# Attention, a dense layer and a mixture of experts: a third expert picked ahead of the full ranking

## The chip, the cores and the metric

The kernel runs on one core of a Trainium2 chip, as one launch. The metric is the device time of that launch in microseconds. A shorter time is better. A profile is one execution of the program recorded by the hardware; its span runs from the first to the last instruction.

## The reference

Three layers follow one another: attention over 2 x 8 heads of 768 x 64, a dense layer of 512 -> 2048 -> 512 on 1536 tokens, and a mixture of 8 experts of 512 -> 1024 -> 512, in which each token goes to one expert.

```python
scores_l = where(|i - j| < 16, q @ k.T / 8, -1e9)         # local keys
scores_s = q @ max_of_32(k).T / 8 + log(32)               # 24 summary keys
x = softmax([scores_l, scores_s]) @ [v, mean_of_32(v)]    # -> [1536, 512]

h = x @ w_in                                              # dense layer
x = (h * clip(h + 3, 0, 6) / 6) @ w_out

e = argmax(x @ w_gate); p = softmax(x @ w_gate)[e]        # expert of each token
out = p * (maximum(x @ w1[e], 0) @ w2[e])
```

All data are float32. The kernel writes each product of float32 matrices as three products of float16 halves (high x high, high x low, low x high).

## The kernel before, in words

The work is one long program for five engines, with the order of most steps planned by hand: `POS` and the second argument of `at` give each step a position, and the steps are traced in that order. A scheduler then places the instructions in each engine's program; inside `tc.manual_schedule` the order on the named engines is the written one. A `tc.If` is a conditional block; each engine that has instructions in it evaluates the condition itself, and jumps past the block when it is false.

Attention and the dense layer take the first 377 us. The dense layer's first matmuls are L486 (weights `wih`, `wil`), its second ones L506 (`wo`); `x2_out` stores the result of 128 tokens and transposes it, and `gate` (L526 to L571) picks the expert of each token and writes the token's number into that expert's table `tbl`.

The experts are worked through by rank, the most frequented first. `early` looks at the counts of the first 8 of the 12 token tiles (`PRE`) and fixes the experts of ranks 0 and 1, so that their weights can be loaded and split while the dense layer still runs. `ranking` orders all eight once every token is counted, with the experts picked early kept in front. `s_tile(v, j)` computes tile j (128 tokens, or 64 in a half tile) of rank v: L709 with `w1`, relu on ACT (L713) and the low half on DVE (L714), L728 (L724 in a half tile) with `w2`, the scaling by p (L731, L733) and a scatter to `out` (L734).

Weights come in pieces of 512 KB, eight to an expert (four of `w1`, four of `w2`). `s_load` brings a piece into a raw buffer, by a DMA on SP's queue (L655, L658); `s_split` makes the high half on ACT (L193) and the low half on DVE (L194). Up to the ranking there are three raw buffers (`eraw`), behind it five (`raw`, `RAW`); a load into a buffer follows the split that frees it. Pieces 8 v + i of ranks 0 and 1 are steps `sw0` to `sw15`. Rank 2 and later ranks are prepared by `prep`, four pieces at a time, as `work` inside `s_tile`: there the order on ACT and DVE is written, relu, low half, relu, low half, then the pieces. Rank v's weights lie in pair `v % 4` of `sp["w"]`; two pairs (`w1t`, `w2t`) exist early, two more (`w1u`, `w2u`) are made behind the dense layer.

The order behind the dense layer is: tiles (0,0), (0,1), (0,2) of rank 0, whose rows were gathered early; then a block L876 (`redo`) for the case that rank 0 has fewer tiles than were worked ahead; the half tile of rank 0 if it has one; a nest of blocks L867 with further tiles of rank 0; tile (1,0); a nest L867 with further tiles of rank 1, in the first of which the pieces of ranks 2 to 4 are prepared; then the other ranks. Each tile's tokens come by a gather on GpSimd (L679) and a transposing DMA on SP's queue (L681); each table by a DMA on SP's queue (L673, L784).

In the profiled execution rank 0 has three tiles and a half tile, rank 1 seven tiles, rank 2 a tile and a half tile, ranks 3 and 4 a half tile each.

Of the kernel before, what the change touches and what calls it, by code (L numbers as in the profile page):

```python
# [20 lines left out]
NT = B * S  # L21
# [10 lines left out]
RAW = 5  # L32

# [116 lines left out]
def attn_moe_moe2(ctx, tc, q, k, v, w_in, w_out, w_gate, w1, w2, cf_d, ch_d, out):  # L150
# [17 lines left out]

    wctx = ExitStack()
# [18 lines left out]
    wih = wpool.tile([128, KD, DFF], F16, name="wih")  # L188
    wil = wpool.tile([128, KD, DFF], F16, name="wil")
# [390 lines left out]
    esc = const.tile([1, 5], F32, name="esc")  # L580
    esi = const.tile([1, 4], I32, name="esi")
    early_tiles = [(0, 1), (0, 2)]
    z0, z1 = ew[:, 0, :], ew[:, 1, :]

    def early():

        n, c = ew[:, 2, :], ew[:, 3, :]
        ve.tensor_copy(n, counts(PRE))
        for i, z in enumerate((z0, z1)):
            ve.tensor_reduce(out=esc[:, i:i + 1], in_=n, axis=AX.X, op=ALU.max)  # L590
            ve.scalar_tensor_tensor(out=c, in0=n, scalar=esc[:, i:i + 1], in1=rev[0:1], op0=ALU.is_ge, op1=ALU.mult)
            ve.tensor_reduce(out=esc[:, 2 + i:3 + i], in_=c, axis=AX.X, op=ALU.max)
            ve.tensor_scalar(out=z, in0=rev[0:1], scalar1=esc[:, 2 + i:3 + i], scalar2=None, op0=ALU.is_equal)
            if i == 0:
                ve.scalar_tensor_tensor(out=n, in0=z, scalar=-BIG, in1=n, op0=ALU.mult, op1=ALU.add)
        ve.tensor_scalar(out=esc[:, 2:4], in0=esc[:, 2:4], scalar1=-1.0, scalar2=float(E), op0=ALU.mult, op1=ALU.add)
        ve.tensor_copy(esi, esc[:, 0:4])
        ve.tensor_scalar(out=esi[:, 0:1], in0=esi[:, 0:1], scalar1=7, scalar2=None, op0=ALU.logical_shift_right)
        ve.tensor_scalar(out=esc[:, 4:5], in0=esi[:, 0:1], scalar1=float(len(early_tiles) + 1), scalar2=None, op0=ALU.min)
        return esi  # L600

    def ranking(up):
# [13 lines left out]
        for i, z in enumerate((z0, z1)):  # L616
            ve.scalar_tensor_tensor(out=o, in0=z, scalar=float(2 - i) * 2 * E * NT, in1=o, op0=ALU.mult, op1=ALU.add)
# [21 lines left out]
        ve.scalar_tensor_tensor(out=resi[:, 1:2], in0=esc[:, 4:5], scalar=float(1 << 20), in1=wd[:, 1:2],  # L639
# [97 lines left out]
    def s_open():  # L737
# [5 lines left out]
                   for i in range(2)]  # L743
        xg = {vj: fp.tile([128, 2 * KD, 128], F16, name=f"xe{vj[0]}{vj[1]}") for vj in [(0, 0)] + early_tiles}
# [6 lines left out]
    def tiles_max(v):  # L751

        n, late = PRE * 128, NT - PRE * 128
        if v < 2:
            n = n // (v + 1) + late
        else:
            n = (n * (v - 1) // (v + 1) + late) // (v - 1)
        return -(-n // 128)

    def sparse():  # L760
# [4 lines left out]
        sp["w"] += [(fb.tile([128, 2, KD, FF], F16, name=f"w1u{i}"), fb.tile([128, 2, FK, DM], F16, name=f"w2u{i}"))  # L765
                    for i in range(2)]
# [24 lines left out]
        def raw_loads(first, *gs):  # L791
            with tc.issue_after(first.ins):
                for g in gs:
                    s_load(2, g)
# [18 lines left out]
        def prep(r, half):  # L813

            def piece(i):
                s_split(r, i)
                g = 8 * r + i + RAW
                if g < 8 * E:
                    s_load(g // 8, g % 8)
            return [lambda i=i: piece(i) for i in range(4 * half, 4 * half + 4)]  # L820

        def prep_x(r):
            gather(r, 0)
            h_gather(r)
            if r + 1 < E:
                t_load(r + 1)
                h_load(r + 1)
# [3 lines left out]
        for vj in early_tiles:  # L831
            s_tile(*vj, work=prep(2, 0) if vj == early_tiles[-1] else ())
# [5 lines left out]
        beside = 5  # L838

        def prep_now(r, half):  # L840
            if half == 0 or r == 2:
                prep_x(r)
            for f in prep(r, half):
                f()

        def full(v, j):

            gather(v, j + (2 if v == 1 else 1))
            if (v, j) == (1, 0):
                h_gather(1)  # L850
            if v == 1 and j < beside:
                r, h = 2 + (j + 1) // 2, (j + 1) % 2
                if h == 0 or r == 2:
                    prep_x(r)
                s_tile(v, j, work=prep(r, h))
            else:
                s_tile(v, j)
# [24 lines left out]
        last_half(0)  # L882
        chain(0, n)
# [4 lines left out]
        with tc.If(nt[1] <= 2 * beside - 1):  # L888
            for j in range(1, beside):
                with tc.If(nt[1] <= 2 * j + 1), tc.If(nt[2 + (j + 1) // 2] > 0):  # L890
                    prep_now(2 + (j + 1) // 2, (j + 1) % 2)
        with ExitStack() as st:  # L892
            for v in range(2, E):
# [4 lines left out]
                if v + 3 < E:  # L898
                    with tc.If(nt[v + 3] > 0):  # L899
                        for half in range(2):  # L900
                            prep_now(v + 3, half)
# [118 lines left out]
    def s_early():  # L1020
# [3 lines left out]
        sp["e"] = [reg(esi[0:1, 2 + i:3 + i], E - 1, (ET.SP,)) for i in range(2)]  # L1024
# [7 lines left out]
    def s_early_w(v, i):  # L1032
        s_split(v, i)
        n = 8 * v + i + 3
        if n < 16:
# [3 lines left out]
    for n in range(16):  # L1039
        at(111.9 + n // 2, f"sw{n}", lambda n=n: s_early_w(n // 8, n % 8))  # L1040
# [11 lines left out]
    s_tile(0, 0)  # L1052
# [37 lines left out]
```

## Time and profile before

| what | value |
|---|---|
| median of 3 runs | 565.24 us (558.17 to 565.33) |
| the profiled execution's own time | 560.59 us |
| its span | 558.7 us |
| TensorE (PE) busy | 475.8 us, 85% of the span |
| VectorE (DVE) busy | 304.1 us, 54% |
| ScalarE (ACT) busy | 264.1 us, 47% |
| GpSimd (POOL) busy | 223.3 us, 40% |
| DMA traffic | 87.46 MB, 157 GB/s on average |
| mean granted TensorE clock | 0.928 of full speed |

Sums of a term are made against the profiled execution. A share of busy time is an average over stages; a stage is read by its own window.

### The profile page before, as it was taken

What the parts mean: (1) busy time and instruction counts of PE and PEld (TensorE: products, weight loads), DVE (VectorE), ACT (ScalarE), POOL (GpSimd) and SP (SyncE); (2) the same over time, 40 slices, a digit from 0 to 9 for tenths busy, and PEclk for the clock granted to TensorE, in tenths of its full rate; (3) what the DMA queues carried; (4) which work ended last, traced back from release to release, by engine and by line L of the source; (5) the groups of instructions that cost most, each with busy time, mean ns of one, the idle gap of its engine ahead of it and who ended that gap; (6) DMA issues with size and microseconds to landing.
All of it is one profiled execution on the core that took longest, in us unless ns stands there. A gap on an engine that the chain in (4) does not pass through costs nothing. (4 is left out here: it accounts for less than half of the span.)

```text
span 558.7 us, 12697 instructions
## 1 busy us (share of the span) xinstructions
PE 475.8 (85%) x4792; PEld 324.4 (58%) x4792; DVE 304.1 (54%) x772; ACT 264.1 (47%) x559; POOL 223.3 (40%) x217
## 2 busy tenths in 40 slices
PE   6726966959989999999999997999978969986971
PEld 2325854737656554597578566637745737754650
DVE  5999699996992233645154338954242446320110
ACT  3777685776874213447165406642142346320120
POOL 3476666775675112456245405612213213120110
PEclk8856896898999999999999999999989989997996
DMA  8997977996641354533532348861476999970210
GB/s 272 265 253 192 326 202 161 212 219 181 181 108 34 76 95 105 106 98 58 114 67 50 58 138 248 259 204 40 167 160 172 237 284 328 239 245 22 46 34 7
DMA packets 114773, 87.46 MB, mean 157 GB/s; under 512 B 85199, under 2 KB 94671, under 8 KB 114688
## 3 DMA queue, kind: packets, MB, share of 16 engines
q1 hardware_dynamic: 104656, 65.27, 47.9%
q10 hardware_dynamic: 7056, 13.11, 7.9%
q0 software_dynamic: 2976, 8.01, 4.3%
q8 instruction: 46, 0.75, 0.6%
q14 instruction: 39, 0.32, 0.2%
HBM read 57.29 MB, written 7.97 MB: 117 GB/s over the span
## 5 line engine op out<-in xcount | busy, mean ns | idle before, releaser
L486 PE MATMUL hps<-xt,wih 128*128 128x256 f16 x768 | 136.2, 282 | 9.2 <-DVE rel L492 4.6
L506 PE MATMUL x2ps<-wo,gt 128*128 128x512 f16 x576 | 131.6, 380 | 1.3 <-POOL gt L497 1.1
L486 PE MATMUL hps<-xt,wil 128*128 128x256 f16 x384 | 108.1, 282 | 2.8 <-POOL wil L243 2.8
L506 PEld LDWEIGHTS <-gt 128*128 128x128 f16 x576 | 54.7, 98 | 62.3 <-POOL gt L497 1.6
L486 PEld LDWEIGHTS <-wih 128*128 128x128 f16 x768 | 76.2, 101 | 23.6 <-issue 3.8
L497 POOL TENSOR_TENSOR gt<-rel,gt 128x512 f16<-128x512 f32 x48 | 56.5, 1185 | 39.8 <-ACT gt L496 37.0
L709 PEld LDWEIGHTS <-w1t 128*128 128x128 f16 x1152 | 61.8, 100 | 11.8 <-DVEq L876 4.6
L728 PE MATMUL yp<-w2t,hh 128*128 128x512 f16 x240 | 55.8, 387 | 7.2 <-ACT hh L713 7.0
L714 DVE SCALAR_TENSOR_TENSOR hh<-hp,hh 128x512 f16<-128x512 f32 (+1 forms) x30 | 18.4, 618 | 68.5 <-ACT hh L713 68.4
L492 DVE SCALAR_TENSOR_TENSOR rel<-rel,hps 128x512 f32<-128x512 f32 x48 | 32.6, 680 | 27.9 <-ACT rel L491 27.7
L407 ACT ACTIVATE s<-s,nm 128x184 f32<-128x184 f32 x88 | 38.2, 435 | 19.1 <-DVE nm L402 18.5
L728 PEld LDWEIGHTS <-hh 128*128 128x128 f16 x264 | 25.3, 99 | 36.7 <-ACT hh L713 7.4
L486 PEld LDWEIGHTS <-wil 128*128 128x128 f16 x384 | 38.8, 101 | 10.9 <-POOL wil L243 2.9
L491 ACT ACTIVATE rel<-hps,brelu 128x512 f32<-128x512 f32 x48 | 32.5, 677 | 19.6 <-PE hps L486 14.3
L713 ACT ACTIVATE hh<-hp 128x512 f16<-128x512 f32 (+1 forms) x30 | 16.0, 539 | 54.2 <-PE hp L709 52.3
L709 PE MATMUL hp<-xb,w1t 128*128 128x128 f16 x672 | 38.7, 219 | 1.7 <-DVEq L867 1.7
L496 ACT ACTIVATE gt<-rel 128x512 f16<-128x512 f32 x48 | 29.8, 624 | 20.2 <-DVE rel L492 19.9
L417 POOL TENSOR_TENSOR pb<-s,pb 128x512 f16<-128x512 f32 x22 | 25.9, 1177 | 31.5 <-issue 22.7
L734 POOL DMA_INDIRECT out_dram<-y,tb x8 | 9.2, 1146 | 62.2 <-ACT y L731 40.8
L381 PEld LDWEIGHTS <-qt 64*128 64x128 f16 x576 | 18.6, 100 | 24.3 <-issue 8.8
L569 POOL DMA_INDIRECT tbl<-row,slot x12 | 12.8, 1069 | 45.6 <-DVE slot L563 44.8
L381 PE MATMUL ps<-kb,qt 64*128 64x160 f16 x288 | 19.1, 254 | 10.4 <-DVE nm L397 8.3
(180 smaller groups left out, 783.9 us busy)
## 6 DMA issues: line engine op xcount, KB each, us to landing
raw<-in_moe_w_dram SPq DMA_DIRECT2D x29, 512.0 KB, 6.2
stg<-in_moe_w_out_dram ACTq DMA_DIRECT2D x16, 512.0 KB, 4.2
eraw<-in_moe_w_dram SPq DMA_DIRECT2D x16, 512.0 KB, 4.2
stg<-in_moe_w_in_dram ACTq DMA_DIRECT2D x9, 512.0 KB, 5.0
x2d<-x2c SPq DMA_DIRECT2D x12, 256.0 KB, 2.5
vraw<-in_v_dram SPq DMA_DIRECT2D x11, 256.0 KB, 3.6
qraw<-in_q_dram SPq DMA_DIRECT2D x10, 256.0 KB, 3.6
ek<-in_k_dram SPq DMA_DIRECT2D x3, 512.0 KB, 6.4
```

The lines of the kernel that those rows point to most:

```text
L381: nc.tensor.matmul(out=ps[i % 2][:, o + c0:o + c1], lhsT=qt[u][p, a, h // 2, :], rhs=keys[p, c, h // 2, :], start=(j == 0), stop=(j == 2))
L407: nc.scalar.activation(s[:, i, :], s[:, i, :], AF.Exp, bias=nm[:, i:i + 1], accum_out=sums[u][:, 4 * g + i:4 * g + i + 1])
L417: nc.gpsimd.tensor_tensor(out=p[:, :, 256:384], in0=s[:, :, 0:c1], in1=p[:, :, 0:c1], op=ALU.subtract)
L486: nc.tensor.matmul(out=hps[:, c, :], lhsT=w[:, kk, f:f + 128], rhs=xt[j][:, a * KD + kk, :], start=(i == 0), stop=(i == 3 * KD - 1))
L491: nc.scalar.activation(r, hf, AF.Relu, scale=S_G / (S_X * S_WI) ** 2, bias=brelu)
L492: nc.vector.scalar_tensor_tensor(out=r, in0=r, scalar=6.0 * S_G / (S_X * S_WI), in1=hf, op0=ALU.min, op1=ALU.mult)
L496: nc.scalar.activation(gh, r, AF.Copy)
L497: nc.gpsimd.tensor_tensor(out=gl, in0=r, in1=gh, op=ALU.subtract)
L506: nc.tensor.matmul(out=o, lhsT=gts[j][:, a, f, i * 128:(i + 1) * 128], rhs=w[:, f, :], start=(f == 0 and n == 0), stop=(f == KF - 1 and n ...
L709: nc.tensor.matmul(out=hp[:, c, :], lhsT=w1t[:, a, kk, f:f + 128], rhs=x[:, b * KD + kk, 0:n], start=(i == 0), stop=(i == 3 * KD - 1))
L714: ve.scalar_tensor_tensor(out=hh[:, 1, m * 4:m * 4 + 4, :], in0=hp, scalar=0.0, in1=hi, op0=ALU.max, op1=ALU.subtract)
L728: nc.tensor.matmul(out=yp, lhsT=hh[:, a, f, :], rhs=w2t[:, b, f, :], start=(f == 0 and i == 0), stop=(f == FK - 1 and i == 2))
```

## The change

`EARLY = 3` experts are picked from the counts of the first 8 token tiles instead of 2. The third one's weights go into the space of `wih` and `wil`, which the dense layer's first matmuls have read for the last time by then (they move to a pool of their own, `wi`, that stays open); one pair `w1u`, `w2u` is made later instead of two. Of its eight pieces, 16 and 17 are steps `sw16`, `sw17` behind `sw15`, 18 to 21 are the `work` of tile (0,0), and 22 and 23 (`SOON` = 22) that of tile (0,2), which had 16 to 19. Pieces 24 to 26 are prepared between rank 0's half tile and the nest L867 of rank 0. The rank-1 tiles (1,0) to (1,4) then prepare 3, 3, 3, 2 and 2 pieces, where each had four. The gathers for ranks 2, 3 and 4 are begun in (1,0), (1,1) and (1,3) as before.

```diff
+EARLY = 3
+SOON = 8 * (EARLY - 1) + 6
...
+    wi = ctx.enter_context(tc.tile_pool(name="wi", bufs=1))
...
-    wih = wpool.tile([128, KD, DFF], F16, name="wih")
-    wil = wpool.tile([128, KD, DFF], F16, name="wil")
+    wih = wi.tile([128, KD, DFF], F16, name="wih")
+    wil = wi.tile([128, KD, DFF], F16, name="wil")
...
-    z0, z1 = ew[:, 0, :], ew[:, 1, :]
+    zs = [ew[:, i, :] for i in range(EARLY)]
...
-        for i, z in enumerate((z0, z1)):
+        for i, z in enumerate(zs):
             ve.tensor_reduce(out=esc[:, i:i + 1], in_=n, axis=AX.X, op=ALU.max)
...
-            if i == 0:
+            if i < EARLY - 1:
                 ve.scalar_tensor_tensor(out=n, in0=z, scalar=-BIG, in1=n, op0=ALU.mult, op1=ALU.add)
...
-        for i, z in enumerate((z0, z1)):
-            ve.scalar_tensor_tensor(out=o, in0=z, scalar=float(2 - i) * 2 * E * NT, in1=o, op0=ALU.mult, op1=ALU.add)
+        for i, z in enumerate(zs):
+            ve.scalar_tensor_tensor(out=o, in0=z, scalar=float(EARLY - i) * 2 * E * NT, in1=o, op0=ALU.mult, op1=ALU.add)
...
+        sp["w"].append([t.rearrange("p k f -> p (k f)").rearrange("p (a k f) -> p a k f", a=2, k=k)
+                        for t, k in ((wih, KD), (wil, FK))])
...
-        sp["w"] += [(fb.tile([128, 2, KD, FF], F16, name=f"w1u{i}"), fb.tile([128, 2, FK, DM], F16, name=f"w2u{i}"))
-                    for i in range(2)]
+        sp["w"].append((fb.tile([128, 2, KD, FF], F16, name="w1u"), fb.tile([128, 2, FK, DM], F16, name="w2u")))
...
-                    s_load(2, g)
+                    s_load((SOON + g) // 8, (SOON + g) % 8)
...
-        def prep(r, half):
-
-            def piece(i):
-                s_split(r, i)
-                g = 8 * r + i + RAW
-                if g < 8 * E:
-                    s_load(g // 8, g % 8)
-            return [lambda i=i: piece(i) for i in range(4 * half, 4 * half + 4)]
+        def prep(lo, hi):
+
+            def piece(g):
+                s_split(g // 8, g % 8)
+                if g + RAW < 8 * E:
+                    s_load((g + RAW) // 8, (g + RAW) % 8)
+            return [lambda g=g: piece(g) for g in range(lo, hi)]
...
-            s_tile(*vj, work=prep(2, 0) if vj == early_tiles[-1] else ())
+            s_tile(*vj, work=prep(SOON, 8 * EARLY) if vj == early_tiles[-1] else ())
...
-        beside = 5
+        beside = [8 * EARLY + i for i in (3, 6, 9, 12, 14, 16)]
+        first = {0: 2, 1: 3, 3: 4}
...
-            if v == 1 and j < beside:
-                r, h = 2 + (j + 1) // 2, (j + 1) % 2
-                if h == 0 or r == 2:
-                    prep_x(r)
-                s_tile(v, j, work=prep(r, h))
+            if v == 1 and j < len(beside) - 1:
+                if j in first:
+                    prep_x(first[j])
+                s_tile(v, j, work=prep(beside[j], beside[j + 1]))
...
         last_half(0)
+        for f in prep(8 * EARLY, beside[0]):
+            f()
         chain(0, n)
...
     def s_early_w(v, i):
         s_split(v, i)
         n = 8 * v + i + 3
-        if n < 16:
+        if n < SOON:
             s_load(n // 8, n % 8)
...
-    for n in range(16):
-        at(111.9 + n // 2, f"sw{n}", lambda n=n: s_early_w(n // 8, n % 8))
+    for n in range(SOON - 4):
+        at(111.9 + n // 2 if n < 8 * (EARLY - 1) else 120.9 + n % 8, f"sw{n}", lambda n=n: s_early_w(n // 8, n % 8))
...
-    s_tile(0, 0)
+    s_tile(0, 0, work=[lambda n=n: s_early_w(n // 8, n % 8) for n in range(SOON - 4, SOON)])
```

## Rows read from the trace of the kernel before

**Rows 1.** Busy time by window, whole core; granted clock, DMA share and GB/s last.

```profile
377.50:396.00 18.50, 18.50 (x250) 14.48 (x247) 9.63 (x56) 4.20 (x10) 2.96 (x3) 1.00 0.16 44
414.00:423.50 9.50, 7.84 (x112) 5.69 (x112) 1.59 (x3) 1.46 (x3) 0.98 (x1) 0.83 0.50 108
```

**Rows 2.** TensorE's timeline: start, us, instructions, idle before and its releaser.

```profile
354.96 0.27 PE L486 MATMUL hps<-xt,wil 128*128 128x256 f16 x1
...
382.87 0.44 PE L533 MATMUL pl<-wg,x2t 128*128 128x8 f16 x12
...
404.56 5.34 PE L728 MATMUL yp<-w2t,hh 128*128 128x512 f16 x24
...
414.00 4.39 PE L709 MATMUL hp<-xh,w1t 128*128 128x64 f16 x96 [4.09 <-DVEq L876]
423.50 5.53 PE L709 MATMUL hp<-xb,w1t 128*128 128x128 f16 x96 [1.66 <-DVEq L867]
...
454.97 6.89 PE L728 MATMUL yp<-w2t,hh 128*128 128x512 f16 x24 [4.85 <-ACT hh L713]
...
490.49 0.61 PE L728 MATMUL yp<-w2t,hh 128*128 128x512 f16 x2 [2.19 <-ACT hh L713]
491.29 4.92 PE L728 MATMUL yp<-w2t,hh 128*128 128x512 f16 x22 [0.19 <-DVE hh L714]
...
540.51 2.96 PE L709 MATMUL hp<-xh,w1t 128*128 128x64 f16 x96 [1.71 <-DVEq L867]
```

**Rows 3.** ACT's timeline, 411 to 486 us, columns as above.

```profile
411.45 0.67 ACT L731 ACTIVATE y<-yp,tbe 128x512 f32<-128x512 f32 x1
...
447.47 1.06 ACT L193 ACTIVATE w1u<-raw 128x1024 f16<-128x1024 f32 x1 [6.31 <-DMA raw<-in_moe_w_dram]
...
454.33 1.08 ACT L713 ACTIVATE hh<-hp 128x512 f16<-128x512 f32 x2
...
485.31 1.06 ACT L193 ACTIVATE w2t<-raw 128x1024 f16<-128x1024 f32 x1 [5.97 <-DMA raw<-in_moe_w_dram]
```

**Rows 4.** SP's queue, 378 to 441 us: when each DMA was issued.

```profile
378.81 1.23 SPq L519 DMA_TRANSPOSE x2t<-x2c  x1
...
420.63 0.41 SPq L658 DMA_DIRECT2D raw<-in_moe_w_dram  x1
...
440.15 1.19 SPq L655 DMA_DIRECT2D raw<-in_moe_w_dram  x1
```

**Rows 5.** SP's own waits, 390 to 500 us: us in total, times, longest.

```profile
SPq L681 <- DMA xr<-x2d,tb: 29.6, 6, 7.6
```

**Rows 6.** DVE's timeline, 324 to 423 us, columns as above.

```profile
324.84 0.15 DVE L590 TENSOR_REDUCE esc<-ew 1x1 f32<-1x8 f32 x1
...
325.71 0.15 DVE L595 SCALAR_TENSOR_TENSOR ew<-ew 1x8 f32<-1x8 f32 x1
...
357.95 3.27 DVE L194 SCALAR_TENSOR_TENSOR w1t<-eraw,w1t 128x1024 f16<-128x1024 f32 x1 [0.26 <-ACT w1t L193]
...
374.65 1.23 DVE L194 SCALAR_TENSOR_TENSOR w2t<-eraw,w2t 128x1024 f16<-128x1024 f32 x1 [0.82 <-ACT w2t L193]
...
390.15 0.15 DVE L614 COPY rw<-pc 1x8 f32<-1x8 f32 x1 [1.68 <-PE pc L575]
...
406.34 2.36 DVE L194 SCALAR_TENSOR_TENSOR w1u<-raw,w1u 128x1024 f16<-128x1024 f32 x2 [0.26 <-ACT w1u L193]
...
411.58 1.23 DVE L194 SCALAR_TENSOR_TENSOR w1u<-raw,w1u 128x1024 f16<-128x1024 f32 x1 [0.20 <-ACT w1u L193]
...
422.65 0.74 DVE L733 SCALAR_TENSOR_TENSOR y<-yp,tbh,y 64x512 f32<-64x512 f32 x1 [3.38 <-ACTq L867]
```

**Rows 7.** DMA issues of the page: KB each, median us to landing.

```profile
raw<-in_moe_w_dram SPq DMA_DIRECT2D x29, 512.0 KB, 6.2
...
eraw<-in_moe_w_dram SPq DMA_DIRECT2D x16, 512.0 KB, 4.2
```

More of the change, by code (lines that the diff above doesn't have):

```diff
@@ L638, in ranking @@
         ve.tensor_copy(resi[:, 0:1], wd[:, 0:1])
-        ve.scalar_tensor_tensor(out=resi[:, 1:2], in0=esc[:, 4:5], scalar=float(1 << 20), in1=wd[:, 1:2],
+        ve.scalar_tensor_tensor(out=resi[:, 1:2], in0=esc[:, 2 * EARLY:], scalar=float(1 << 20), in1=wd[:, 1:2],
                                 op0=ALU.mult, op1=ALU.add)
@@ L753, in tiles_max @@
         n, late = PRE * 128, NT - PRE * 128
-        if v < 2:
+        if v < EARLY:
             n = n // (v + 1) + late
         else:
-            n = (n * (v - 1) // (v + 1) + late) // (v - 1)
+            k = v - EARLY + 1
+            n = (n * k // (v + 1) + late) // k
         return -(-n // 128)
@@ L836, in sparse, with prep_now @@
         done = nc.snap(words[1] >> 20)
-        beside = 5
-        def prep_now(r, half):
-            if half == 0 or r == 2:
-                prep_x(r)
-            for f in prep(r, half):
+        beside = [8 * EARLY + i for i in (3, 6, 9, 12, 14, 16)]
+        first = {0: 2, 1: 3, 3: 4}
+        def prep_now(j):
+            if j in first:
+                prep_x(first[j])
+            for f in prep(beside[j], beside[j + 1]):
                 f()
@@ L850, in full @@
                 h_gather(1)
-            if v == 1 and j < beside:
-                r, h = 2 + (j + 1) // 2, (j + 1) % 2
-                if h == 0 or r == 2:
-                    prep_x(r)
-                s_tile(v, j, work=prep(r, h))
+            if v == 1 and j < len(beside) - 1:
+                if j in first:
+                    prep_x(first[j])
+                s_tile(v, j, work=prep(beside[j], beside[j + 1]))
             else:
@@ L887, in sparse @@
         last_half(1)
[L888 to L891, printed above, removed]
+        with tc.If(nt[1] <= 2 * len(beside) - 3):
+            for j in range(1, len(beside) - 1):
+                with tc.If(nt[1] <= 2 * j + 1), tc.If(nt[3 if j == 1 else 4] > 0):
+                    prep_now(j)
         with ExitStack() as st:
@@ L899, in sparse @@
                     with tc.If(nt[v + 3] > 0):
-                        for half in range(2):
-                            prep_now(v + 3, half)
+                        prep_x(v + 3)
+                        for f in prep(8 * (v + 3), 8 * (v + 4)):
+                            f()
     ek = [mp.tile([128, 4, HP, 256], F32, tag="g", name="ek") for _ in range(2)]
@@ L1023, in s_early @@
         early()
-        sp["e"] = [reg(esi[0:1, 2 + i:3 + i], E - 1, (ET.SP,)) for i in range(2)]
+        sp["e"] = [reg(esi[0:1, EARLY + i:EARLY + i + 1], E - 1, (ET.SP,)) for i in range(EARLY)]
         for i in range(3):
```

18 lines of the change are left out of this document (10 added, 8 removed).

## Prediction, made before the change was run

> **What bounds the kernel now.** I read the stages by windows first, then TensorE's own timeline, then the engines that release it. In the last of the dense layer, between 377.5 and 396, TensorE is busy in all 18.5 us, with the DMA engines at 0.16 [rows 1]. After 409.9 the rank-0 and rank-1 tiles run, and there TensorE stands still four times [rows 2]: 4.09 us ahead of rank 0's half tile at 414.00, 1.66 us ahead of the first rank-1 tile at 423.50, 4.85 us before 454.97 and 2.19 us before 490.49. The reader is to see who releases each. The last two wait for ACT's relu (L713), and ACT was not working: in its program order the splits of the weight pieces stand ahead of the next tile's relu, and a split waited 6.31 us for its raw data at 447.47 and 5.97 us at 485.31 [rows 3]. The data were late because SP issued them late, at 440.15 [rows 4]: SP takes its instructions in order and stood 29.6 us in six waits for gathers behind which its transposes queue [rows 5]. The first two stops are of another kind. The releaser is DVE's sequencer passing a conditional block (L876, L867): the buffers of the next matmuls are also used inside the skipped block, so TensorE goes on only when ACT and DVE have each come to that block and stepped over it. At L876 DVE came late because its last split started at 411.58 and lasted 1.23 us; at L867 it had just done the half tile's output, 422.65 plus 0.74 [rows 6].
>
> **What the change does to each.** Call a piece one 512 KB load and its split, numbered 8 x rank + i. Before, pieces 0 to 15 are done in the dense layer's tail, 16 to 19 in tile (0,2), 20 to 39 four to a tile in (1,0) to (1,4). After, pieces 0 to 17 and then 18 to 21 (beside tile (0,0)) are done early, 22 and 23 in (0,2), 24 to 26 between the half tile and the block at L867, then 3, 3, 3, 2 and 2 in the rank-1 tiles. The total stays 40.
>
> *The stops in rank 1.* With three or two pieces a tile, six loads fewer go through SP's queue after the ranking, and five raw buffers stand two or more pieces ahead of use. In (1,1) the pieces 30 and 31 have been issued before that tile's gathers; piece 32 is the one issued about 440, as piece 25 was, but it is the last of the three and not the second of four. The 4.85 us go, and with them the lower clock of the matmuls behind: 24 of them took 6.89 us, where 24 take 5.34 at 404.56 [rows 2], so 1.55 more. In (1,4) the two pieces' loads stem from (1,2); the 2.19 us go. Sum -8.6 us. What is late next is piece 35: its load waits behind the gathers of (1,1), and if (1,3) starts earlier it may hold ACT's relu there: 0 to +2 us, I take +1.
>
> *The stop at L876.* DVE's two splits there end at 406.34 + 2.36 = 408.7 [rows 6], before TensorE's last matmul at 409.90 [rows 2]. ACT is then last: its output instruction, which started at 411.45 behind the splits [rows 3], follows the matmuls directly, and DVE's 1.2 us from the end of its last split (412.81) to the matmuls at 414.00 is the price of reading the counts and stepping over, which ACT pays too. 409.9 plus some 2.3 gives 412.2: -1.8 us. The half tile's 96 matmuls took 4.39 us after the 4.09 us of rest and the same form takes 2.96 at 540.51 [rows 2], the granted clock of 414 to 423.5 being 0.83 [rows 1], so part of it ran at the 1.2 GHz level; the shorter rest I put beside the one of 2.19 us before 490.49, behind which the stretch kept its pace, and take that back: -1.4. Sum -3.2 us; the half tile then ends at 418.7.
>
> *The three pieces ahead of L867.* This is the added wait. Queued behind them on ACT and DVE is the step over L867, and TensorE waits for both. The bounds are far apart and hang on where the scheduler, which the source doesn't bind here, puts the pieces. (a) All three ahead of the block: piece 26 uses the load that SP issued at 420.63 [rows 4]; the raw loads land after a median of 6.2 us, those of the early stage after 4.2 [rows 7]. With 4.4, since it is alone in its queue, its ACT split starts at 425.0, its DVE split ends at 425.0 + 1.06 + 1.23 = 427.3, and the tile (1,0) starts there and not at 423.50: 8.6 us of rest against 1.66, +7, and +1.5 for the clock. (b) Pieces 24 and 25 ahead, 26 behind: the half tile's output ends on DVE at 420.3, two DVE splits of 1.23 end at 422.9: 4.2 us of rest, +2.6, and +1.5 for the clock, together +4.1. (c) All behind: 0. I take (b), because SP's order shows that instructions whose data come late sink behind such a block (the load at 420.63 stands ahead of L876 in the source, and is issued while the half tile behind that block already runs [rows 2, 4]), and 26 is the only late one. The Trainium skill, "DMA: Bandwidth & Descriptors", section "Anatomy of one DMA — SWDGE (gpsimd) path", gives about 2.0 us plus the bytes at 436 GB/s. As an estimate that is 3.2 us for a piece, and (a) would be 1.2 us cheaper by it; this trace disagrees, with medians of 4.2 and 6.2 us.
>
> *The dense tail.* Six more pieces and one more round of the choice: five DVE instructions of 0.15 to 0.22 us (the five from 324.84 to 325.71 [rows 6]), one register for SP, one more instruction in the ranking, all ahead of loads that have slack, so I cost the latter three at nothing, hidden by the matmuls to 409.9; without that cover they are about 1.3 us. The eight pieces 8 to 15 start their DVE splits from 357.95 to 374.65, so 2.4 us each [rows 6]; six more end about 390, over 6 us ahead of the loads that reuse the space. The DMA engines have room there, 0.16 [rows 1]. What may touch TensorE: the transposes of the last dense tile (378.81) land beside loads instead of alone and feed the router product at 382.87 [rows 2, 4]; and DVE's ranking at 390.15 may stand behind one split of 1.23. Lower bound 0, upper +4, I take +1: TensorE has other tiles' matmuls around these. Writing the third expert's weights over the dense first layer's needs no wait: its last matmul starts at 354.96 [rows 2], and piece 16 comes behind piece 15, at 374.65 on DVE.
>
> Sum for (b): -8.6 + 1 - 3.2 + 4.1 + 1 = -5.7 us, from the profiled execution's 560.59 to 554.9. That execution lies 4.65 below the median of the three runs and 2.42 above the lowest. I put half of the 4.65 on top: 557.
>
> **The rivals.** All in the profiled execution's terms. *Piece 26 holds L867* (a): -8.6 - 3.2 + 8.5 + 1 = -2.3, 558.3. For it: the source order, and nothing else for ACT to do. Against: the sinking of late loads. *The pieces sink* (c): -8.6 + 1 - 3.2 + 1 = -9.8, 550.8. *Slower: piece 21 holds the ranking, and so piece 26.* Its raw buffer is freed by piece 18, whose split is written behind the second relu of tile (0,0), so its load goes out near 386.4; landing after 6.2 us, its ACT split starts at 392.6 and its DVE split ends at 394.9. If the ranking stands behind that on DVE, it starts there and not at 390.15, 4.7 us late, and the chain from it over the table load, the gather and the transposes to load 26 moves with it. With piece 26 ahead of L867 the tile (1,0) then starts at 432.0 and not at 423.50: +8.5 + 1.5 - 8.6 + 1 = +2.4, 563.0. The point from which it decides: data of piece 26 later than 427.3. For it: the written order in tile (0,0), and load 440.15 whose split started 7.3 us later [rows 3, 4]. Against: the DMA engines are free there, and at 4.2 us the load lands in time. The Trainium skill, "DMA: Bandwidth & Descriptors", in the same section, says that a DMA waits for a semaphore on the issuing sequencer, before dispatch; by that, load 21 on SP would also hold what is queued behind it until piece 18 is split. The waits of [rows 5] agree; it has the same sign and price as this rival. *Nothing moves*: the loads stay late behind SP's gathers with fewer pieces too, and what L876 gives L867 takes: about 560.
>
> **How the numbers follow.** (b) 0.37, (a) 0.25, (c) 0.18, slower 0.13, nothing 0.07. Two per cent, 11.2 us, is about what a measurement of this kernel can tell from no change. Faster by over that needs (c) and a cheap tail: half of (c) and a little of (b), 0.14. Slower by over it needs a stop that is in none of the cases, or the slow rival with a landing near 14 us: 0.06. The rest, 0.80, is within. The range reaches from (c), less the 2.42 us to the lowest run, about 549, to the slow rival, plus the 4.65 us to the median, about 567; it leaves out little, and takes in the bounds of L867 and of the tail.
>
> **What would show it.** After: no rest of TensorE over 1 us between the second rank-1 tile and the last; ACT's split waits for raw data under 3 us in (1,1) and (1,4); TensorE released at L876 by ACT and not DVE, after some 2.3 us; at L867 a rest of about 4 us with two splits between the half tile's output and the step over it. A rest of 8 us there is (a), 1.7 is (c). DMA activity in the window from 377.5 to 396 up from 0.16 to some 0.5, with the matmuls there unbroken. I am wrong if a new rest appears ahead of 410, if L867 costs more than L876, (1,1) and (1,4) give, or if the raw loads still come after the relus.

## The result, and the profile after

The changed kernel takes 564.77 us in the median of 20 executions (560.64 to 569.29), the kernel before 562.24 in 20 measured beside it (556.66 to 567.16). The ratio is 1.0078, with a 95% interval of 1.0051 to 1.0104: slower by about three quarters of a per cent, where 557 and a small gain were forecast. The profiled execution has a span of 566.0 us, against 558.7. A ratio counts only executions within 1.5% of a kernel's lowest and so is no quotient of the medians (it lies 0.5 to 0.9% above it for e4, e8, e9, e10 and e11 below, and 0.6% below it for e1), and the profiled executions of e1 and e7 lay outside that bound. No ratio in this document reaches the 2 per cent that the prediction took for what a measurement can tell from no change, so the argument rests on stages of the profiles, with ratios and intervals beside them.

I read the new trace as the old one. First the windows of the whole core: the stretch, its length, the busy time of PE, PEld (weight loads), DVE, ACT and POOL, and granted clock, DMA share and GB/s last. They are the router stage behind the dense layer, the stretch to the end of tile (0,2), the half tile with what stands around it, and rank 1.

```profile
377.50:396.00 18.50, 16.28 (x174) 11.73 (x173) 11.35 (x33) 7.93 (x13) 1.02 (x1) 0.91 0.74 206
384.70:388.00 3.30, 3.30 (x41) 3.30 (x42) 2.66 (x9) 0.43 (x1) 0.00 (x0) 0.50 0.94 364
388.10:396.00 7.90, 7.90 (x112) 6.24 (x111) 4.39 (x20) 3.78 (x7) 1.02 (x1) 1.00 0.49 113
396.00:420.42 24.42, 23.49 (x242) 15.53 (x237) 11.90 (x38) 7.23 (x12) 6.05 (x6) 1.00 0.38 123
420.42:438.17 17.75, 8.34 (x114) 6.20 (x113) 4.04 (x5) 4.25 (x6) 1.97 (x2) 0.81 0.83 144
...
438.17:517.56 79.39, 74.70 (x840) 53.68 (x841) 26.01 (x28) 26.29 (x35) 22.91 (x21) 1.00 0.83 223
```

The first window was full before, at a granted clock of 1.00 and a DMA share of 0.16 [rows 1]. Now TensorE is idle there for 2.2 us, the clock is 0.91 and the DMA share 0.74; the lower clock lies in one piece, 0.50 (the 1.2 GHz level) from 384.70 to 388.00, right behind that rest. Rank 1 is the good news: 79.39 us, where it was 86.97 (423.50 to the next expert's half tile at 510.47 in the trace before). TensorE's own timeline says what stops it (idle time before, and its releaser, in brackets):

```profile
384.67 0.48 PE L537 MATMUL pl<-wg,x2t 128*128 128x8 f16 x12 [2.22 <-DMA x2t<-x2c]
385.02 4.32 PE L715 MATMUL hp<-xe,w1t 128*128 128x128 f16 x49
...
389.23 2.73 PE L715 MATMUL hp<-xe,w1t 128*128 128x128 f16 x46
...
428.17 4.88 PE L715 MATMUL hp<-xh,w1t 128*128 128x64 f16 x96 [7.75 <-DVEq L886]
...
438.17 5.53 PE L715 MATMUL hp<-xb,w1t 128*128 128x128 f16 x96 [1.66 <-DMA xa<-xr]
...
476.46 0.60 PE L734 MATMUL yp<-w2t,hh 128*128 128x512 f16 x2 [0.33 <-ACT hh L719]
```

Against [rows 2]: the router product of the last token tile but one waits 2.22 us for its transposes, which it did not before, and the 49 matmuls behind take 4.32 us where the next 46 take 2.73. The rest ahead of rank 0's half tile has grown from 4.09 to 7.75 us. The one ahead of the first rank-1 tile is 1.66 as it was. Both stops inside rank 1 are gone; the largest rest left there is the 0.33 us at 476.46. Next SP's queue, when it issued what:

```profile
376.36 2.78 SPq L661 DMA_DIRECT2D eraw<-in_moe_w_dram  x2
379.39 1.26 SPq L523 DMA_TRANSPOSE x2t<-x2c  x1
...
395.89 0.38 SPq L664 DMA_DIRECT2D eraw<-in_moe_w_dram  x1
407.50 0.59 SPq L793 DMA_DIRECT2D tbh<-tbl  x1
409.01 0.34 SPq L679 DMA_DIRECT2D tb<-tbl  x1
409.90 0.97 SPq L664 DMA_DIRECT2D raw<-in_moe_w_dram  x2
...
418.81 0.91 SPq L661 DMA_DIRECT2D raw<-in_moe_w_dram  x2
```

The loads 16 and 17 go out right ahead of the transposes that the router waits for (the last ones stood alone at 378.81 before, [rows 4]). Load 21 goes out at 395.89, the loads 22 and 23 at 409.90, 24 and 25 at 418.81. DVE and ACT show what held them:

```profile
401.14 1.23 DVE L198 SCALAR_TENSOR_TENSOR wil<-eraw,wil 128x1024 f16<-128x1024 f32 x1 [2.16 <-ACT wil L197]
402.56 0.15 DVE L620 COPY rw<-pc 1x8 f32<-1x8 f32 x1 [0.19 <-DVE wil L198]
...
423.53 1.23 DVE L198 SCALAR_TENSOR_TENSOR w1u<-raw,w1u 128x1024 f16<-128x1024 f32 x1 [3.39 <-ACT w1u L197]
425.76 1.23 DVE L198 SCALAR_TENSOR_TENSOR w1u<-raw,w1u 128x1024 f16<-128x1024 f32 x1 [1.00 <-ACT w1u L197]
```

```profile
400.05 1.06 ACT L197 ACTIVATE wil<-eraw 128x1024 f16<-128x1024 f32 x1 [3.31 <-DMA eraw<-in_moe_w_dram]
...
422.44 1.06 ACT L197 ACTIVATE w1u<-raw 128x1024 f16<-128x1024 f32 x1 [1.25 <-DMA raw<-in_moe_w_dram]
424.67 1.06 ACT L197 ACTIVATE w1u<-raw 128x1024 f16<-128x1024 f32 x1 [1.17 <-DMA raw<-in_moe_w_dram]
...
440.03 1.06 ACT L197 ACTIVATE w1u<-raw 128x1024 f16<-128x1024 f32 x1 [2.75 <-SPq L877]
...
462.87 1.06 ACT L197 ACTIVATE w1t<-raw 128x1024 f16<-128x1024 f32 x1 [3.52 <-DMA raw<-in_moe_w_dram]
...
474.28 1.06 ACT L197 ACTIVATE w1t<-raw 128x1024 f16<-128x1024 f32 x1 [6.92 <-DMA raw<-in_moe_w_dram]
```

The ranking begins at 402.56, released by the DVE split of piece 21 that ended at 402.37; it began at 390.15 before [rows 6]. The loads 22 to 25 come behind the ranking on SP. Pieces 24 and 25 stand ahead of L886 on both engines, wait there for their data, and DVE steps over the block only when its split has ended at 425.76 + 1.23 = 426.99; TensorE goes on 1.2 us later. Piece 26 sank behind L877 (440.03).

**One table for all kernels.** The instruction order of every kernel up to the early choice is the same, and yet the time of that part wanders by up to 5 us from one profiled execution to the next. So I compare by stage, between four instants of TensorE: the start of its last second-layer matmul of the dense layer (A, 377.00 us before), the end of tile (0,2) (B, 409.91), the start of rank 1 (C, 423.50) and the start of the next expert's half tile (D, 510.47). Each entry is the kernel's stage less that of before, in us, from one profiled execution each; the last column is the median less that of before measured beside it, over 4 to 20 executions.

| kernel | up to A | A to B, router | B to C, half tile | C to D, rank 1 | medians |
|---|---|---|---|---|---|
| changed | +5.1 | +5.4 | +4.1 | -7.6 | +2.5 |
| e1, none between | +2.0 | +6.1 | +1.5 | -6.1 | +0.4 |
| e2, pieces 16 to 21 out | -3.2 | +0.9 | +1.0 | -6.5 | -7.3 |
| e3, only their loads out | -1.7 | +3.5 | +1.8 | -5.7 | -1.9 |
| e5, piece 21 out | -2.5 | +4.4 | +0.6 | -5.4 | -1.8 |
| e4, before, two beside (0,2) | -0.8 | +1.0 | +1.9 | +9.4 | +6.1 |
| e7, e1 with 21 moved | +0.9 | +4.9 | -0.8 | +2.1 | +0.3 |
| e8, third pick only | -0.1 | +1.1 | +1.1 | -1.3 | +0.7 |
| e9, ranking first | -1.2 | +1.9 | -0.3 | +0.1 | -1.5 |
| e10, spread over seven | -0.3 | +0.7 | -0.5 | -6.3 | -9.2 |
| e11, e4 without the redo block | -4.6 | +0.9 | -4.6 | +10.6 | +0.6 |

An entry is good to about 1 us: e4, e10 and e11 do nothing new between A and B, e8 only the third pick, and they show +0.7 to +1.1 there. For the changed kernel the stages behind A give 5.4 + 4.1 - 7.6 and another 0.4 from D to TensorE's last matmul, together +2.4 before rounding, and the medians +2.5. The 5.1 ahead of A are no effect of it: 4.9 of them stand already at the middle of the first dense product (at 236 us in the kernel before), ahead of every changed instruction, where the ten others show -3.8 to +1.1.

### The profile page after: what moved, and what is told of

It reads as the page before. It is cut to its first block, busy times and chain, and to the rows that moved or that the text cites. A ratio compares the mean times of both kernels' runs of the same rounds, so it can differ in the third digit from the quotient of the medians.

```text
span 566.0 us, 12705 instructions
## 1 busy us (share of the span) xinstructions
PE 476.8 (84%) x4792; PEld 325.5 (58%) x4792; DVE 301.2 (53%) x778; ACT 263.3 (47%) x559; POOL 223.9 (40%) x217
## 4 chain that ended last, share of the span: by engine, by line
PE 39%; DMA 27%; DVE 17%; issue 9%; ACT 3%; POOL 1%; SPq 1%; POOLq 0%; another core or an unknown queue 0%; ACTq 0%; DVEq 0%
PE x2ps L510 16%; PE hps L490 11%; DMA xr<-x2d,tbh 7%; PE hp L715 5%; DMA xr<-x2d,tb 3%; PE yp L734 3%; DMA tbl<-row,slot 3%; DMA stg<-in_moe_w_in_dram 3%; DMA pt<-pb 2%; DVE yps L234 2%; DVE y L238 2%; DVE yps L236 2%; DVE s L401 2%; DVE kb L198 2%; PE ps L385 2%
## 5 line engine op out<-in xcount | busy, mean ns | idle before, releaser
L715 PEld LDWEIGHTS <-w1t 128*128 128x128 f16 x1152 | 63.8, 102 | 16.2 <-DVEq L886 8.2
L443 PE MATMUL po<-vt,pt 128*128 128x64 f16 x264 | 15.9, 199 | 14.4 <-DMA pt<-pb 10.5
```

The lines of the kernel that those rows point to most:

```text
L715: nc.tensor.matmul(out=hp[:, c, :], lhsT=w1t[:, a, kk, f:f + 128], rhs=x[:, b * KD + kk, 0:n], start=(i == 0), stop=(i == 3 * KD - 1))
```

## The experiments

My theory after the result: the six pieces ahead of the ranking cost TensorE some 5 us up to B, and by way of a late ranking and late loads some 4 us more at the half tile; rank 1 gave what it should. Rivals: the third pick itself costs; the pieces between half tile and L877 are the loss; the earlier stage is the loss (the table rules that out).

**e1: the three pieces between go to rank 1.**

```diff
-        beside = [8 * EARLY + i for i in (3, 6, 9, 12, 14, 16)]
+        beside = [8 * EARLY + i for i in (0, 4, 7, 10, 13, 16)]
...
-        for f in prep(8 * EARLY, beside[0]):
-            f()
```

> The changed kernel with pieces 24 to 26 moved from between the half tile and L877 into the rank-1 tiles (4, 3, 3, 3, 3 pieces). Theory (the scheduler puts pieces 24 and 25 ahead of the block L886, where their raw loads come late): ACT and DVE reach L886 with only the splits of 22 and 23 done, the rest of TensorE ahead of the half tile falls from 7.75 us to 2.5 to 3, the half tile's matmuls take 3.0 us and not 4.9, so 5 to 7 us less than the changed kernel and a ratio to the kernel before of 0.995 to 0.998, if the tiles of rank 1 take the moved pieces without a stop. Rival (the 4.9 us that the changed kernel's profile has lost at 340 us, in the attention stage with the same instruction order, are the loss, and the pieces cost nothing net): the same 4.9 us at 340 us and a ratio of 1.005 or more.

562.23 us in the median, before 561.79; ratio 0.9948 (0.9900 to 0.9996). With no split ahead of it the wait at L886 falls to 0.97 us, and a new stop stands 34 matmuls into the half tile, which the profile puts down to "issue", time in which the engine waits for nothing that it shows:

```profile
418.93 1.15 PE L715 MATMUL hp<-xh,w1t 128*128 128x64 f16 x34 [0.97 <-PEq L886]
424.42 3.48 PE L715 MATMUL hp<-xh,w1t 128*128 128x64 f16 x62 [4.34 <-issue]
```

So the pieces between are worth 4.1 - 1.5 = 2.6 us of the half-tile stage, but the stage does not become shorter than before, and rank 1 gives back 1.5 us for them. The router stage is unchanged at +6.1, and the ranking starts again 0.19 us behind the split of piece 21:

```profile
398.89 0.15 DVE L620 COPY rw<-pc 1x8 f32<-1x8 f32 x1 [0.19 <-DVE wil L198]
```

**e2: pieces 16 to 21 are left out; e3: their loads alone; e5: piece 21 alone.** All three leave weights of the third expert unprepared, e3 splits stale data in their place.

```diff
 e2:
-        if n < SOON:
+        if n < 16:
...
-    for n in range(SOON - 4):
+    for n in range(16):
...
-    s_tile(0, 0, work=[...])
+    s_tile(0, 0)
 e3: the first of these alone
 e5:
-        if n < SOON:
+        if n < SOON - 1:
```

> The changed kernel without pieces 16 to 21: neither their loads nor their splits are made, so rank 2 uses what its weight tiles held. Theory (loads beside the transposes of the last dense tiles, and a ranking that waits for piece 21): no wait of over 0.5 us ahead of the router products, TensorE at the end of tile (0,2) 5 to 6 us earlier than in the changed kernel from 340 us on, ranking and loads 22 to 25 earlier by 8 to 9 us, the rest at L886 about 4 us as before the change. 8 to 10 us less than the changed kernel: ratio to the kernel before 0.985 to 0.99. Rival (attention stage): the tail gives nothing, ratio 1.005 or more. A third view, that what costs is the time of the splits on ACT and DVE and not the loads, says the same here and parts from the theory in the run with the loads alone left out.

> The changed kernel with the six loads of pieces 16 to 21 left out and their splits kept, which read what the raw buffers hold. Theory (the loads are the cause): within 1.5 us of the run without the pieces. If ACT's and DVE's time for the splits is the cause, the ranking and the rest at L886 stay as in the changed kernel, within 2 us of its time. Rival (attention stage): as the changed kernel, ratio 1.005 or more.

> The changed kernel without piece 21 alone (load and split left out), the only one whose load waits for a split behind the relus of tile (0,0). Theory: the router product's wait of 2.2 us stays; the ranking starts without waiting for that load and ends some 3 to 4 us earlier against TensorE, loads 22 to 25 too, and the rest at L886 falls from 7.75 to some 4 us; 3 to 5 us less than the changed kernel, ratio to the kernel before 0.998 to 1.003. If the other splits hold the ranking as well, it gains under 1.5 us. Rival (attention stage): as the changed kernel.

Medians 554.54, 559.86 and 560.03, with 561.79 before; ratios 0.9887 (0.9815 to 0.9958), 0.9984 (0.9946 to 1.0023) and 0.9990 (0.9949 to 1.0032). Without the pieces the router stage is back at +0.9, the half tile at +1.0, and the rank-1 gain of 6.5 us stays: with the six pieces not prepared at all the change is worth 7 us, more than a kernel that prepares them elsewhere could have. By the medians the six cost 2.5 + 7.3 = 9.8 us, the loads 4.5 of it, piece 21 4.3; by the stages behind A 7.6, 3.3 and 3.3. Piece 21's part is the ranking, which in e5 starts behind the count matmul and not behind a split, 0.2 us later than before once the router product's own shift (+0.5) is taken off:

```profile
390.88 0.15 DVE L620 COPY rw<-pc 1x8 f32<-1x8 f32 x1 [1.03 <-PE pc L579]
```

The loads alone don't explain the router stage, as the theory had it: e3 keeps +3.5 there, with splits only. Its router product waits just 0.85 us, and about 2 us lie in two rests of 0.92 and 1.02 us inside tile (0,2), again put down to issue. Rests of 0.98 to 1.00 are at that place in e1, e5 and e7 too, smaller ones (0.28 to 0.75) in the changed kernel, e2, e4, e8, e10 and e11, none in the kernel before; what they are I did not settle.

**e4: the kernel before with two pieces beside (0,2).**

```diff
-            s_tile(*vj, work=prep(2, 0) if vj == early_tiles[-1] else ())
+            s_tile(*vj, work=prep(2, 0)[0:2] if vj == early_tiles[-1] else ())
...
-                s_tile(v, j, work=prep(r, h))
+                s_tile(v, j, work=prep(r, h, -2) if j == 0 else prep(r, h))
```

> The kernel before with only pieces 16 and 17 beside tile (0,2); pieces 18 and 19 go to the first tile of rank 1, which then has six. Dense tail and ranking are as before. The prediction's step (the stop at L876, 4.39 us, loses 1.8 us of wait and 1.4 us of clock): the half tile starts about 3 us earlier against the tile (0,2) ahead of it, and rank 1 gives back 4 to 6 us for the two pieces more, so 1 to 3 us slower than before. Rival, that another stop takes the place of the wait (as the 4.34 us put down to issue in the run with no pieces between): the half tile starts no earlier than in before, within 0.5 us against the end of (0,2), and the kernel is 4 to 6 us slower than before.

568.80 us, before 562.70; ratio 1.0160 (1.0090 to 1.0230). This is the prediction's step at L876 done alone, in the kernel before:

```profile
411.57 1.15 PE L709 MATMUL hp<-xh,w1t 128*128 128x64 f16 x34 [1.47 <-DVEq L877]
416.50 3.49 PE L709 MATMUL hp<-xh,w1t 128*128 128x64 f16 x62 [3.78 <-issue]
...
425.65 5.53 PE L709 MATMUL hp<-xb,w1t 128*128 128x128 f16 x96 [1.66 <-DVEq L868]
...
452.18 1.03 PE L728 MATMUL yp<-w2t,hh 128*128 128x512 f16 x2 [10.17 <-ACT hh L713]
```

The half tile starts 2.4 us earlier, as the step had it, and rank 1 2.2 us later than before: a stop 34 matmuls into the half tile takes the place of the wait. The rival was right about the stop, though not that the half tile would start no earlier. TensorE itself jumps past the block at the end of (0,2) in both kernels (line, engine, operation, count, shortest/median/longest duration in ns, first and last start in us):

```profile
L876 PEldq COMPARE_BRANCH  x1: 423/423/423, 409.5 to 409.5; - x1
```

```profile
L877 PEldq COMPARE_BRANCH  x1: 516/516/516, 410.1 to 410.1; - x1
```

The first line is of the kernel before, the second of e4. In e4 the 35th matmul starts at 416.50, 6.4 us behind the jump; in the kernel before, where 34 of 96 matmuls that took 4.39 us together follow 414.00, I estimate it at some 6 us behind its jump, without a stop. So the wait for DVE, as I read it, covered the stop. In rank 1 the six pieces beside the first tile make a stop of 10.17 us in the second, where the kernel before had none; its 4.85 us [rows 2] stood in the third.

**e7: e1 with piece 21 beside (0,2), then 4, 4, 3, 3, 3.**

```diff
-SOON = 8 * (EARLY - 1) + 6
+SOON = 8 * (EARLY - 1) + 5
...
-            s_tile(*vj, work=prep(SOON, 8 * EARLY) if vj == early_tiles[-1] else ())
+            s_tile(*vj, work=prep(SOON, SOON + 2) if vj == early_tiles[-1] else ())
...
-        beside = [8 * EARLY + i for i in (0, 4, 7, 10, 13, 16)]
+        beside = [8 * EARLY + i for i in (-1, 3, 7, 10, 13, 16)]
...
```

> The changed kernel with no pieces between the half tile and rank 1 (as in e1) and piece 21 moved from tile (0,0) to tile (0,2): 18 to 20 beside (0,0), 21 and 22 beside (0,2), the other 17 as 4, 4, 3, 3, 3 in rank 1. If the pieces in the dense tail are the cost and add up (piece 21 alone 3.4 us in e5, from 340 us on), it is 3 us less than e1 up to the half tile and 0 to 2 us of that goes to the fourth piece in rank 1: 558 to 561 us, ratio to before 0.990 to 0.997. If piece 21 cost only because pieces 24 and 25 stood ahead of L886 behind it, e1 has that gain already and this run is equal to e1, 561 to 563 us. If the stop put down to issue after L886 is the same in every kernel without pieces there, it shows again with 4 us.

563.01 us, before 562.70; ratio 1.0008 (0.9952 to 1.0063): by the medians equal to e1. Up to rank 1 the gain did add up: the stages from A to C cost 4.1 us, where they cost 7.6 in e1. But rank 1 took it back, and not with 0 to 2 us: two tiles in a row with four pieces bring its stop back, and its stage goes from -6.1 to +2.1; the stop put down to issue is there for the third time, 34 matmuls in, with half the price:

```profile
416.78 1.15 PE L715 MATMUL hp<-xh,w1t 128*128 128x64 f16 x34 [1.03 <-DVEq L886]
...
419.87 3.18 PE L715 MATMUL hp<-xh,w1t 128*128 128x64 f16 x62 [1.94 <-issue]
...
460.16 7.55 PE L734 MATMUL yp<-w2t,hh 128*128 128x512 f16 x24 [4.99 <-ACT hh L719]
```

**e8: the third pick without its pieces.** Pieces 0 to 15 early, four beside (0,2), four in each of five rank-1 tiles, as before.

```diff
-SOON = 8 * (EARLY - 1) + 6
+SOON = 8 * (EARLY - 1)
...
-        beside = [8 * EARLY + i for i in (3, 6, 9, 12, 14, 16)]
+        beside = [8 * EARLY + i for i in (-4, 0, 4, 8, 12, 16)]
...
-    for n in range(SOON - 4):
+    for n in range(16):
...
-    s_tile(0, 0, work=[...])
+    s_tile(0, 0)
```

> Of the change only the third expert picked early and the weights' place; the pieces lie as in before: 0 to 15 in the dense tail, four beside (0,2), four in each of five rank-1 tiles. If the loss is the pieces in the dense tail, this is the kernel before within 0.5% (ratio 0.997 to 1.004), with the L876 stop (4.4 us) and the rank-1 stop (4.9 us) back. If the third pick itself (six short vector operations ahead of the router's last tiles) or the new place of the weights costs, the router product of the last token tile is 2 us or more later against 340 us than in before, and the ratio is 1.004 to 1.01.

563.43 us, before 562.70, in the medians, which is 0.1%; ratio 1.0070 (1.0032 to 1.0107), and the two don't agree. The sign named for the rival, a router product 2 us late, is not there: it comes at +0.1 and the ranking at 390.28. I take the third pick itself as about nothing, up to 0.7% by the ratio.

**e9: the ranking first.** The loads 16 to 18 wait on SP for the last transposes, DVE's halves of their splits for the ranking; 19 to 21 beside (0,2), the rest as 4, 4, 4, 3, 3.

```diff
+            with tc.issue_after(mark["rank"].ins), tc.issue_after(mark["exp"].ins):
+                s_split(2, i)
...
-        resi = ranking(fb)
+        resi = ranking(const)
...
+    at(129.5, "sl", after(("x2t", TILES - 1), lambda: [s_load(2, i) for i in range(3)]))
```

> A version that should beat both: the third expert picked early as in the change, but pieces 16 to 18 alone are loaded ahead of the ranking, behind the transposes of the last token tile on SP, and split behind the ranking on VectorE (beside (0,1)); 19 to 21 beside (0,2); none between half tile and rank 1; the other 18 as 4, 4, 4, 3, 3. The ranking's small tiles lie outside the memory that the early raw pieces leave, so that it waits for none of them. If the pieces' loads and splits ahead of the ranking were the loss, the router and the ranking are as in before (pl product within 1 us of before against 340 us), the half tile starts 1 to 4 us earlier than before and rank 1 keeps a stop of 1 to 3 us: 555 to 559 us, ratio 0.985 to 0.995. If the loss were something else in the tail (the longer early choice, the weights' place), it is no better than e1, 562 us. If a stop put down to issue takes the place of the L886 wait, 559 to 561 us.

561.23 us, before 562.70; ratio 1.0028 (0.9983 to 1.0073): no better than before. Ahead of rank 1 it does what was meant. The ranking starts at 389.23 and the router and half-tile stages are within 2 us of before. But behind the second of the three tiles with four pieces TensorE stops again (5.07 us before 455.67; a split had waited 7.01 us for its data there), and the gain is gone:

```profile
389.23 0.15 DVE L620 COPY rw<-pc 1x8 f32<-1x8 f32 x1 [1.62 <-PE pc L579]
```

```profile
455.67 4.59 PE L734 MATMUL yp<-w2t,hh 128*128 128x512 f16 x13 [5.07 <-ACT hh L719]
```

**e10: the kernel before, its 20 rank-1 pieces spread over seven tiles.** Rank 1 has seven full tiles with these inputs, and its sixth and seventh held none.

```diff
-        beside = 5
+        spans = [20, 23, 26, 29, 32, 35, 38, 40]
+        beside = len(spans) - 1
+        first = {0: 2, 2: 3, 4: 4}
...
-                s_tile(v, j, work=prep(r, h))
+                s_tile(v, j, work=prep(spans[j], spans[j + 1]))
```

> The kernel before (two experts picked early, 0 to 15 in the dense tail, four pieces beside (0,2)) with the 20 pieces of rank 1 beside its seven full tiles as 3, 3, 3, 3, 3, 3, 2 in place of 4 beside each of the first five. If the stops in rank 1 come from four pieces a tile alone, this has the gain of the change (6 to 8 us between the first tile of rank 1 and the next expert's half tile) with none of its cost ahead of the ranking: 554 to 558 us, ratio to before 0.985 to 0.992. If the gain of the change came from the third expert's weights being ready early, the stops stay and it is equal to before within 0.4%. If the pieces beside the sixth and seventh tile put a new stop there (the weights of ranks 2 to 4 late at the half tiles behind rank 1), the gain is given back there in the same number.

554.16 us, before 563.39; ratio 0.9893 (0.9845 to 0.9942): faster than the kernel before, and with that than the changed one. By the ratio that is 6 us, by the medians 9. All instants up to C lie within 0.4 us of before, and rank 1 is 6.3 us shorter, with the end of the kernel 6.7 us earlier (ACT's longest wait for raw data in rank 1 is 3.32 us, where it was 6.31 [rows 3]):

```profile
413.97 4.35 PE L709 MATMUL hp<-xh,w1t 128*128 128x64 f16 x96 [3.66 <-DVEq L877]
423.43 5.53 PE L709 MATMUL hp<-xb,w1t 128*128 128x128 f16 x96 [1.66 <-DVEq L868]
...
454.07 3.06 PE L728 MATMUL yp<-w2t,hh 128*128 128x512 f16 x12 [0.46 <-ACT hh L713]
...
504.14 0.27 PE L709 MATMUL hp<-xh,w1u 128*128 128x64 f16 x2 [4.01 <-issue]
```

**e11: e4 without the block that redoes the early tiles** (it is skipped with these inputs; other inputs need it).

```diff
-        tc.mark_branch_hint_location("redo", hint="LikelyTaken", engines=[ET.PE])
...
-        with tc.If(done <= len(early_tiles), label="redo"):
-            for _, j in early_tiles:
-                with tc.If(done <= j), tc.If(nt[0] > 2 * j):
-                    gather(0, j)
-                    s_tile(0, j)
```

> The kernel before with two pieces beside (0,2) and six beside the first tile of rank 1, as e4, and without the block that redoes the early tiles (it is skipped with these inputs; left out with it is the correction for other inputs). e4 had a stop of 3.78 us put down to issue, 34 matmuls into the half tile. If that stop is the fetch of TensorE's instructions behind the jump over the block, it is gone here: the half tile runs through from about 411.5 us and rank 1 starts 3 to 5 us earlier against the end of (0,2) than in e4 (15.6 us there), 10.5 to 12.5 us. If it has another cause (the skipped test of the half tile itself, or data), the stop of 3 to 4 us after some 34 matmuls stays, and rank 1 starts 15 us after the end of (0,2). The stop of some 10 us in rank 1 stays either way, and the whole is 562 to 570 us.

563.99 us, before 563.39; ratio 1.0103 (1.0021 to 1.0185); e4's median lay 6.1 above its own before, this one 0.6. Wait and stop at the half tile are both gone, and the 96 matmuls of the half tile run through at 3.22 us:

```profile
406.83 3.22 PE L709 MATMUL hp<-xh,w1t 128*128 128x64 f16 x96 [0.62 <-PE yp L728]
...
415.17 5.53 PE L709 MATMUL hp<-xb,w1t 128*128 128x128 f16 x96 [1.66 <-DVEq L867]
```

From the end of (0,2) to rank 1 it takes 9.0 us, where e4 takes 15.5 and the kernel before 13.6. The skipped block is the cause of both; whether of the stop by its jump or by the hint that goes with it, e11 doesn't tell, as it takes out both. That the 3.8 us are the loading of the instructions behind the jump is my reading of "issue"; no row says it. In rank 1 the stop of the six pieces stays, with 12.35 us.

## Why the prediction was wrong

**The dense tail was mis-sized, and its bounds were too low.** I gave it +1, with an end at +4, "TensorE has other tiles' matmuls around these". It cost 5.4 us up to the end of (0,2) (4.4 to 4.7 against the kernels that change nothing there), and 4.4 to 6.1 in the three other kernels that load and split pieces beside (0,0). The place was right: the transposes beside loads. The router product waited 2.22 us for them, and I had no term for what follows, though I had charged one behind other rests: at a granted clock of 0.50 up to 388.00 the 49 matmuls behind took 4.32 us, 1.4 more than at the pace of the next 46 (49 x 2.73 / 46 = 2.9). Together 3.6 of the 5.4; three rests of 0.20 to 0.33 us inside the tiles make 0.8, and the last 1 us I did not trace. The lower clock is no fixed part of that price, the waits are: in e1 the clock stays at 1.00 behind the same wait, and there the last router product waits for its transposes as well.

```profile
381.60:385.00 3.40, 3.40 (x69) 3.40 (x70) 2.68 (x9) 0.71 (x2) 0.00 (x0) 1.00 0.98 355
```

```profile
381.57 0.46 PE L537 MATMUL pl<-wg,x2t 128*128 128x8 f16 x12 [2.23 <-DMA x2t<-x2c]
...
388.48 0.45 PE L537 MATMUL pl<-wg,x2t 128*128 128x8 f16 x12 [1.08 <-DMA x2t<-x2c]
```

And e3, which makes the splits without the loads, still costs 3.5 us in this stage; I had no term for TensorE behind the splits. The window's DMA share rose to 0.74 and not to some 0.5, and the matmuls there did not stay unbroken.

**The ranking was costed as standing behind at most one split, 1.23 us.** That is the step behind the half tile's price. It started 12.4 us later than before; 8.9 of that had come already at the last router product (5.1 of them ahead of A), and the other 3.5 is piece 21. The slower rival named this mechanism, at 4.7 us, and I gave it 0.13. Its second half was wrong: the late piece that blocked was not 26 at L867, but 24 and 25 at L886. That its sum, +2.4, is the measured one is luck: it has 10.0 us for the two blocks, which cost 4.1, and 1 for the tail, which cost 5.4. What the rival's rule from the Trainium skill says is in the trace as well ("DMA: Bandwidth & Descriptors", section "Anatomy of one DMA — SWDGE (gpsimd) path": a DMA waits for its semaphore on the issuing sequencer): load 21 held SP until piece 18 was split, 6.3 us, here in SP's own waits (us in total, times, longest). Behind it SP had nothing to do until the ranking. (The 3.2 us for a load that the prediction estimated from the same section come from the section's price for DMAs that GpSimd issues; SP issues these, and the rows had 4.2 and 6.2.)

```profile
SPq L656 <- DVE rresi L641: 9.6, 1, 9.6
SPq L664 <- DVE wih L198: 6.3, 1, 6.3
```

**The stop at L876 (-3.2) was not to be had.** I took TensorE to be held by ACT and DVE alone. In e1, e4 and e7, where they are free, TensorE stops 34 matmuls into the half tile for 4.34, 3.78 and 1.94 us; the whole stage went from -0.8 to +1.9 us against before, whatever was freed. e11 shows that the skipped block is behind it. The trace of before had a rest of this kind to ask about, 3.72 us put down to issue ahead of the next expert's half tile, and the working passed it by; it stands there in every kernel here, with 3.6 to 5.6 us:

```profile
510.47 0.48 PE L709 MATMUL hp<-xh,w1u 128*128 128x64 f16 x6 [3.72 <-issue]
```

And in the changed kernel DVE was not free, because pieces 24 and 25 had late data and stood ahead.

**The three pieces ahead of the second block (+4.1) cost nothing at that block.** The rest there stayed 1.66 us, the sign of case (c): piece 26 sank behind it, as the sinking of late loads would have it, but 24 and 25 were taken a block earlier. Together the two blocks were forecast at -3.2 + 4.1 = +0.9 and cost +4.1.

**The stops in rank 1 were right**, -8.6 + 1 = -7.6, and measured -7.6. The next late piece is 35, as the working had it: ACT waits 6.92 us for its data before 474.28, and TensorE stands 0.33 us for the relu behind it, where I took +1. One sign here failed without a price: ACT's wait in (1,1) was to stay under 3 us and was 3.52 (462.87). With three pieces a tile the splits end about when the next relu is due, even where one of them waits that long. e10 shows that this needs no third expert: three a tile is enough, and e7, e8 and e9 that four in tiles one behind the other is not.

The sum: -5.7 was forecast, +2.4 measured behind A. Of the 8.1 between, 4.4 is the tail, 3.2 the two blocks, 0.4 what comes behind rank 1. The measured time lies inside the range because that reached to the slow rival plus the distance to the median; by its own terms the range was 548.4 to 567.7, a little wider than the 549 to 567 written.

## What to carry to other kernels

Before work is moved out of a crowded stage into an earlier one, look for room in the stage itself: here two tiles of rank 1 stood empty, and spreading the same 20 pieces over seven tiles gave 6 to 9 us where moving six pieces ahead of the ranking lost 2.5 by the medians and 4 by the ratio. Work put beside a short chain that feeds everything later (here transposes, router, ranking) is priced by what it delays in that chain and by what hangs on it several stages on, not by how idle the engines look. And a wait that ends last may cover another that ends a moment earlier: before a gain is booked, ask what TensorE would meet next at the same place, a jump over skipped code among it.

## What the runs showed of the hardware that was not expected

A skipped block costs TensorE 6.6 us around a half tile (15.5 us with it in e4, 9.0 without it and its hint in e11), of which the profile shows 3.78 as issue, 34 matmuls behind the jump. In the kernel before, as I read it, a wait of 4.09 us for another engine hid this stop.

The same order of instructions took between 3.8 us less and 4.9 us more than in the one profile of before, up to 236 us. A comparison of two whole profiles would have put that to the change's account; stages told it apart, with medians of 4 to 20 executions beside them.
